# Attention's first batch in two halves, FFN from the 58th step, and a weight fetch moved behind keys

## The chip, the core and the metric

The kernel runs on one core of one Trainium2 chip. The metric is the device time of one execution in microseconds, here the median of three runs. TensorE does the matrix products and the transposes (through an identity matrix), VectorE and ScalarE the elementwise work, GpSimd some elementwise work on data in SBUF, and SyncE (SP) issues nearly all DMAs, in the order of its queue. Each engine runs its own instructions in order.

## What is computed

A sparse attention over 8 batches and 8 heads (each of 512 local positions sees 32 neighbours on both sides and 32 global positions; the global positions see all), and an FFN with an ELU over its 4608 rows.

```python
s_ll = np.where(abs(i - j) <= 32, scale * q_l @ k_l.T, -1e9)
s_l = np.concatenate([scale * q_l @ k_g.T, s_ll], axis=-1)
out_l = sm(s_l) @ np.concatenate([v_g, v_l])          # 512 local rows
out_g = sm(scale * q_g @ k_all.T) @ v_all             # 32 global rows
x = concat([out_g, out_l]).transpose(0, 2, 1, 3).reshape(4608, 512)
h = x @ w_in                                          # 512 -> 2048
g = np.where(h > 0, h, np.exp(np.minimum(h, 0)) - 1)
return g @ w_out                                      # 2048 -> 512
```

Inputs are float32; the FFN weights come as raw 64-bit words and the kernel makes pairs of float16 numbers (a high and a low part) of them. An FFN product is three float16 products: high x high, low x high, high x low.

## The kernel before

**Attention** is a generator. It goes through slots: a "g" slot (`stage_ga`: scores and exponentials of the global rows of one group of four heads) or an "l" slot (a tile: 128 local positions of four heads). For a tile `stage_s` makes the scores (L769 on TensorE, L780 on VectorE with mask and minimum), then exponentials (`ex`, L786, ScalarE) and the norm (L790 and L791 on VectorE, L793 four times on GpSimd, L795 on VectorE). `stage_t` transposes (L809) and copies (L811), `stage_u` transposes the global part (L742 to L745) and copies it (L746, L748, L750 on ScalarE), and `stage_v` multiplies with the values (L853, L822) and copies the result into `xr` (L859 on ScalarE, L864 to L868 on VectorE). Each slot gives four steps. Scores run up to three slots ahead of values. Two "half blocks" of 256 positions make up a batch; `finish` says that one is ready when both groups of heads have their two tiles of that half. A ready half block is split into float16 parts `xh` (L568, ScalarE) and `xl` (L571, VectorE).

**Weights** come in 16 parts of 1 MB (`fetch`, tile `raw`, of which there are two buffers), alternately of w_in (m = 0) and w_out (m = 1). `unit` turns one part into float16: L188 (ScalarE), L189 (GpSimd), L193, L196, L200 (VectorE), L204 (ScalarE, which sums and frees the raw tile), a maximum over partitions (L141), then L213 (ScalarE) and L216 (VectorE). Parts are gathered in groups a (part pair 0), b (1), c (2, 3), d (4 to 7), and f (all 8); `tables` makes a group's scale factors some steps after its last part.

**FFN** is a second generator. A block is done in four jobs by groups a to d while weights are missing, each adding its partial result to an HBM buffer `od` (L440, L459, L455), or in one job f, whose second product uses seven quarter products instead of eight. First product: L324; activation: L333, L334, L335 on ScalarE, L342 on VectorE, split in L349 (ScalarE) and L345 (VectorE); second product: L447 or L482.

What sets the order is a loop over attention's steps with a table of pace: from the step in `PACE[1]` on, FFN pieces (six matmuls each) are put between attention's steps, 180 of them by step 112, 850 by step 320. `UNITS` are the steps at which the first weight parts are started; from eight steps ahead of FFN's start on, credits start the rest. A scheduler then sets the final place of each instruction on its engine, by priorities in that order.

Of the kernel before, what the change touches and what calls it, by code (L numbers as in the profile page):

```python
# [23 lines left out]
NT = SL // P  # L24
# [12 lines left out]
AHEAD = 2  # L37


PACE = ((0, 0), (66, 0), (112, 180), (320, 850))  # L40
WARM = 10
CONV = 14
NBL = B * SL // BLK
GROUPS = {"a": (0, 1), "b": (1, 2), "c": (2, 4), "d": (4, 8), "f": (0, 8)}
BEHIND = 60
UNITS = 0, 1, 8, 18, 30
NX = 4


# [11 lines left out]
def attn_ffn(ctx: ExitStack, tc: tile.TileContext, qT, qgT, kT, vT, vgT, vpT, w_in, w_out, mask, out):  # L61
# [23 lines left out]
    def defer(n, fn):  # L85
        if n == 0:
            return fn()
        later.setdefault(now[0] + n, []).append(fn)
# [49 lines left out]
    def all_max(dst, src):  # L138

        tp = ps_a.tile([P, 512], F32, name="pa")  # L140
        tc.keep_in_program_order(nc.tensor.transpose(tp[:, 0:P], src.to_broadcast([P, P]), ident))  # L141
        nc.vector.tensor_reduce(out=dst, in_=tp[:, 0:P], op=ALU.max, axis=AX.X)
# [15 lines left out]
    def load_weights():  # L158
        todo = [(group, m, p) for group in "abcd" for p in range(*GROUPS[group]) for m in range(2)]
        raws = [fetch(*todo[0][1:])]  # L160
        yield
        for n, (group, m, p) in enumerate(todo):
            if n + 1 < len(todo):
                raws.append(fetch(*todo[n + 1][1:]))
            unit(m, p, raws[n])
            if (m, p) == (1, GROUPS[group][1] - 1):
                defer(12, lambda group=group: tables(group))
                if p == NP - 1:
                    defer(13, lambda: tables("f"))
            yield  # L170

    def fetch(m, p):
        raw = ffn.tile([P, NC, 2 * P, 2] if m == 0 else [P, 2, DM, 2], I32, name="raw")
        nc.sync.dma_start(raw, w1[:, :, 2 * p * P:2 * (p + 1) * P, :] if m == 0 else w2[:, 2 * p:2 * p + 2, :, :])
        return raw
# [51 lines left out]
    def tables(group):  # L227

        r = slice(*GROUPS[group])
        wm = wts.tile([P, 4], F32, name=f"wm_{group}")  # L230
        t = wts.tile([P, NP], F32, name=f"t_{group}")
        nc.vector.tensor_mul(t[:, r], pww[:, r], pwo[:, r])
        nc.vector.tensor_reduce(out=wm[:, 0:1], in_=t[:, r], op=ALU.max, axis=AX.X)

        def rest():
            all_max(wm[:, 1:2], wm[:, 0:1])
            nc.vector.reciprocal(wm[:, 2:3], wm[:, 1:2])
            nc.vector.tensor_scalar(t[:, r], pwo[:, r], wm[:, 2:3], 8.0, ALU.mult, ALU.mult)
            nc.vector.tensor_scalar_mul(isc[:, r], pww[:, r], -2.0 ** -28)
            tab[group] = wm[:, 1:2], t  # L240

        defer(5, rest)
# [417 lines left out]
    def attention():  # L660
# [251 lines left out]

        slots = []
        for b in range(B):
            if b == 0:
                slots += [(*a, *t) for g in range(2) for a, t in [(("g", b, g), ())] + [(("l", b, g), (t,)) for t in range(NT)]]
                continue
            body = [("l", b, g, t) for h in range(2) for g in range(2) for t in (2 * h, 2 * h + 1)]
            slots += [("g", b, 0)] + body[:2] + [("g", b, 1)] + body[2:]
        sts = [{"b": b} for b in range(B)]  # L920
# [28 lines left out]
        for i in range(n + LAGT + 1):  # L949
# [13 lines left out]
            for what in "SVTU" if i < switch else "TSUV":  # L963
# [7 lines left out]
                elif what == "V":  # L971
                    if pairs:
                        b, g, half = pairs.pop()
# [9 lines left out]

    f = ffn_stream()
    units = load_weights()
    done = credit = 0

    def pace(i):
        for (i0, d0), (i1, d1) in zip(PACE, PACE[1:]):
            if i < i1:  # L990
                break
        return d0 + (d1 - d0) * (i - i0) / (i1 - i0)

    def convert(n):
        nonlocal credit
        credit += n
        if credit >= CONV:
            credit -= CONV
            next(units, None)

    for i, _ in enumerate(attention()):
        lead[0] = i < PACE[1][0]
        if i in UNITS:
            next(units)
        elif i >= PACE[1][0] - 8:
            convert(2)
        want = pace(i)
        if lead[0]:
            next(f)
        if done >= want:  # L1010
            tick()
        while done < want:
            if next(f):
                tick()
                break
            done += 1
            convert(1)
            tick()
# [55 lines left out]
```

## Time and profile before

| what | value |
|---|---|
| median of three runs (lowest, highest) | 953.72 us (953.09, 955.16) |
| profiled execution: time, span | 954.72 us, 952.9 us |
| granted TensorE clock, mean | 0.977 |
| busy, TensorE / weight loads | 908.5 us (95%) / 727.8 us (76%) |
| busy, VectorE / ScalarE / GpSimd | 728.1 (76%) / 670.1 (70%) / 271.1 us (28%) |
| HBM read, written | 70.89 MB, 15.20 MB |

Shares of a whole span mix stages with different limits, so the stages are read apart below. In the rows, `x4` behind a form is a count, `[1.5 <-ACT xh L568]` is idle time of the engine ahead of the instruction and the instruction that ended it.

### The profile page before, as it was taken

The numbers are of one execution on the slowest core, as the hardware profiler recorded it, in microseconds if no ns is written. First come the engines' busy times: TensorE is split into PE (matmuls) and PEld (weight loads), VectorE is DVE, ScalarE is ACT, GpSimd is POOL, SyncE is SP. The second block draws the span as 40 slices with busy tenths as digits, with TensorE's granted clock in tenths as the row PEclk, the third lists the DMA queues.
The fourth block names the chain that finished last, engine by engine and source line by source line (L and its number), as shares of the span: only waits on it lengthen the run. The fifth ranks groups of instructions, "written<-read, shape, count | busy, mean of one in ns | idle before, by whom it ended". The sixth has DMA issues, their size and how long they took to land.

```text
span 952.9 us, 23830 instructions
## 1 busy us (share of the span) xinstructions
PE 908.5 (95%) x9216; PEld 727.8 (76%) x9216; DVE 728.1 (76%) x2025; ACT 670.1 (70%) x1584; POOL 271.1 (28%) x483
## 2 busy tenths in 40 slices
PE   6889887899999999999999999999999999999997
PEld 3567564566666788888888888888888888888886
DVE  4988988889967777768776877687777777676566
ACT  5888996776656767757677767677767767666564
POOL 4655481461522322122121212221332312100000
PEclk8779999899999999999999999999999999999999
DMA  6855876331342023101330123102310101000000
GB/s 262 299 179 180 282 224 191 124 123 57 115 157 90 23 100 103 47 26 46 105 121 26 46 78 125 47 27 79 122 49 25 46 23 35 2 23 23 1 24 23
DMA packets 41769, 87.64 MB, mean 92 GB/s; under 512 B 7736, under 2 KB 8888, under 8 KB 41656
## 3 DMA queue, kind: packets, MB, share of 16 engines
q1 hardware_dynamic: 41368, 85.85, 26.6%
q8 instruction: 73, 1.20, 0.5%
q14 instruction: 40, 0.33, 0.1%
q10 hardware_dynamic: 288, 0.26, 0.1%
HBM read 70.89 MB, written 15.20 MB: 90 GB/s over the span
## 4 chain that ended last, share of the span: by engine, by line
PE 67%; DVE 14%; ACT 9%; POOL 3%; issue 3%; DMA 3%; SPq 0%; DVEq 0%; ACTq 0%; POOLq 0%
PE pa L324 25%; PE acc L482 12%; PE h L482 9%; PE acc L447 4%; PE pa L822 3%; PE h L324 3%; PE pa L769 3%; PE pa L809 2%; ACT p L786 2%; DMA raw<-w_out 2%; PE pa L889 2%; DVE gl L345 1%; POOL p L793 1%; DVE cu L196 1%; DVE cu L200 1%
## 5 line engine op out<-in xcount | busy, mean ns | idle before, releaser
L324 PEld LDWEIGHTS <-winh 128*128 128x128 f16 x2160 | 209.4, 98 | 39.2 <-issue 8.4
L793 POOL TENSOR_SCALAR p<-p,sm 128x128 f32<-128x128 f32 x256 | 147.8, 593 | 303.2 <-DVE sm L791 165.0
L324 PE MATMUL pa<-xh,winh 128*128 128x256 f16 x824 | 224.9, 273 | 0.1
L324 PE MATMUL pa<-xl,winh 128*128 128x256 f16 x824 | 224.6, 273 | 0.0
L324 PE MATMUL pa<-xh,winl 128*128 128x256 f16 x824 | 224.6, 273 | 0.0
L361 ACT ACTIVATE gh<-gx,xs 128x896 f16<-128x896 f32 x103 | 107.3, 1042 | 123.1 <-DVE gx L358 123.0
L345 DVE SCALAR_TENSOR_TENSOR gl<-gx,xs,gh 128x896 f16<-128x896 f32 x103 | 119.4, 1159 | 59.9 <-ACT gh L361 59.0
L482 PEld LDWEIGHTS <-gh 128*128 128x128 f16 x1456 | 139.5, 98 | 24.0 <-issue 7.4
L786 ACT ACTIVATE p<-p,m 128x160 f32<-128x160 f32 x256 | 106.7, 421 | 41.6 <-DVE m L780 41.4
L324 PEld LDWEIGHTS <-winl 128*128 128x128 f16 x1080 | 106.1, 98 | 14.3 <-issue 1.2
L333 ACT ACTIVATE g<-pa,xs 128x512 f32<-128x512 f32 x103 | 70.3, 682 | 24.4 <-PE pa L324 23.8
L482 PE MATMUL acc<-wouth,gh 128*128 128x256 f16 x312 | 85.2, 273 | 0.0
L482 PE MATMUL acc<-woutl,gh 128*128 128x256 f16 x312 | 85.1, 273 | 0.0
L335 ACT ACTIVATE g<-g 128x512 f32<-128x512 f32 x135 | 85.0, 630 | 0.1
L482 PE MATMUL acc<-wouth,gl 128*128 128x256 f16 x312 | 85.0, 273 | 0.0
L482 PEld LDWEIGHTS <-gl 128*128 128x128 f16 x728 | 71.2, 98 | 9.2 <-DVE gl L345 1.0
L482 PE MATMUL h<-raw,gh 128*128 128x256 f16 x416 | 75.0, 273 | 0.0
L324 PE MATMUL h<-xh,winh 128*128 128x256 f16 x256 | 71.1, 279 | 1.5 <-ACT hs L334 0.9
L324 PE MATMUL h<-xl,winh 128*128 128x256 f16 x256 | 71.0, 278 | 0.7 <-DVE xl L571 0.7
L324 PE MATMUL h<-xh,winl 128*128 128x256 f16 x256 | 71.0, 278 | 0.0
L780 DVE CUSTOM_DVE_ANT_0 p<-pa,msk 128x160 f32<-128x160 f32 x228 | 61.5, 318 | 4.8 <-PE pa L769 4.7
L342 DVE SCALAR_TENSOR_TENSOR gx<-g,hs 128x512 f32<-128x512 f32 x51 | 35.9, 704 | 36.0 <-ACT g L335 35.6
(236 smaller groups left out, 2016.9 us busy)
## 6 DMA issues: line engine op xcount, KB each, us to landing
k<-kT SPq DMA_DIRECT2D x32, 640.0 KB, 5.1
v<-vT SPq DMA_DIRECT2D x64, 256.0 KB, 2.8
q<-qT SPq DMA_DIRECT2D x32, 256.0 KB, 5.6
raw<-w_in SPq DMA_DIRECT2D x8, 1024.0 KB, 5.9
raw<-w_out SPq DMA_DIRECT2D x8, 1024.0 KB, 6.8
out<-o SPq DMA_DIRECT2D x32, 256.0 KB, 2.3
od<-o SPq DMA_DIRECT2D x24, 256.0 KB, 3.1
o<-od SPq DMA_DIRECT2D x24, 256.0 KB, 2.8
```

The source lines that it names most:

```text
L324: nc.tensor.matmul(h[:, j, :], wt[:, c, f], xt[:, c, :], start=k == 0, stop=k == 11)
L333: nc.scalar.activation(g, hf, AF.Relu, scale=sc[:, p:p + 1])
L335: nc.scalar.activation(g, g, AF.Exp, scale=-1.0)
L342: nc.vector.scalar_tensor_tensor(out=out, in0=ins[0], scalar=-1.0, in1=ins[1], op0=ALU.add, op1=ALU.max)
L345: nc.vector.scalar_tensor_tensor(out=dst, in0=src, scalar=sg, in1=hi, op0=ALU.mult, op1=ALU.subtract)
L361: nc.scalar.activation(gh, gx, AF.Copy, scale=sg)
L447: nc.tensor.matmul(acc[t], gt[:, s], wt[:, f, :], start=p == first and j == 0 and k == 0, stop=p == last and j == 1 and k == 2)
L482: nc.tensor.matmul(cols, gt, w, start=p == 0 and k == 0, stop=last and k == len(todo) - 1, skip_group_check=True)
L769: nc.tensor.matmul(sp[r][half * HQ:(half + 1) * HQ, j * KW:(j + 1) * KW], q[rows, qs], k[rows, t, half, :], start=True, stop=True)
L780: nc.vector.tensor_tensor_reduce(out=p, in0=sp[r][:, j * KW:(j + 1) * KW], in1=msk[:, mi, :], op0=ALU.add, op1=ALU.min, scale=-scale, scal ...
L786: nc.scalar.activation(ps[i], ps[i], AF.Exp, bias=m[:, i:i + 1], scale=-1.0, accum_out=s[:, 0, i:i + 1])
L793: nc.gpsimd.tensor_scalar(ps[i][:, 0:P], ps[i][:, 0:P], s[:, 1, i:i + 1], 1.0, ALU.mult, ALU.mult)
```

## The change

Attention's first batch did its two groups of heads one after the other, four tiles each. Now it goes like the others: two tiles of the first group, two of the second (first half), then the same for the second half. FFN starts at step 58 instead of 66, weight parts are started at steps 0, 5, 9, 18, 30, and the scale tables are made four steps later after their group's last part.

```diff
-PACE = ((0, 0), (66, 0), (112, 180), (320, 850))
+PACE = ((0, 0), (58, 0), (112, 180), (320, 850))
...
-UNITS = 0, 1, 8, 18, 30
+UNITS = 0, 5, 9, 18, 30
...
-                defer(12, lambda group=group: tables(group))
+                defer(16, lambda group=group: tables(group))
                 if p == NP - 1:
-                    defer(13, lambda: tables("f"))
+                    defer(17, lambda: tables("f"))
...
         for b in range(B):
-            if b == 0:
-                slots += [(*a, *t) for g in range(2) for a, t in [(("g", b, g), ())] + [(("l", b, g), (t,)) for t in range(NT)]]
-                continue
             body = [("l", b, g, t) for h in range(2) for g in range(2) for t in (2 * h, 2 * h + 1)]
             slots += [("g", b, 0)] + body[:2] + [("g", b, 1)] + body[2:]
```

What stands on the queue of SP right after the mask's load, before the change (`raw` are weight parts, `v` values, `q` queries, `k` keys, `qg` global queries, `ptw2` the global values of a group):

```order
L174 DMA raw_164<-w_in 128x4x512
L174 DMA raw_166<-w_out 128x2x1024
L688 DMA ptw2_83<-vpT 128x256
L681 DMA v_200<-vT 128x512
L681 DMA v_237<-vT 128x512
L676 DMA qg_254<-qgT 128x64
L666 DMA k_256<-kT 128x1280
L666 DMA k_258<-kT 128x1280
L174 DMA raw_231<-w_in 128x4x512
```

and after it:

```order
L174 DMA raw_164<-w_in 128x4x512
L676 DMA qg_174<-qgT 128x64
L666 DMA k_176<-kT 128x1280
L666 DMA k_178<-kT 128x1280
L688 DMA ptw2_83<-vpT 128x256
L681 DMA v_197<-vT 128x512
L174 DMA raw_199<-w_out 128x2x1024
L671 DMA q_219<-qT 128x512
L671 DMA q_221<-qT 128x512
L681 DMA v_240<-vT 128x512
L174 DMA raw_242<-w_in 128x4x512
```

The second weight part has moved behind the second group's keys, and that group's queries, which stood behind the third part, now stand ahead of it.

ScalarE from the first tile's exponentials (`p1_94`) on, before; `p2_95` and `p0_93` are the second and the third tile:

```order
L786 ACTIVATE p1_94,sm_193<-p1_94,m_192 128x160 x4
L188 ACTIVATE cu_168<-raw_164 128x1024
L786 ACTIVATE p2_95,sm_226<-p2_95,m_225 128x160 x4
L786 ACTIVATE p0_93,sm_271<-p0_93,m_270 128x160 x2
L188 ACTIVATE cu_233<-raw_166 128x1024
L786 ACTIVATE p0_93,sm_271<-p0_93,m_270 128x160 x2
L746 COPY ptw0_81<-pa_289 64x4x32
L748 COPY ptw0_81<-pa_289 64x4x32
L750 COPY ptg0_84<-pa_289 128x2x64
L786 ACTIVATE p1_94,sm_320<-p1_94,m_319 128x160
L204 ACTIVATE raw_164,cm_169<-cu_168 128x1024
```

and after:

```order
L786 ACTIVATE p1_94,sm_191<-p1_94,m_190 128x160 x4
L188 ACTIVATE cu_201<-raw_164 128x1024
L786 ACTIVATE p2_95,sm_234<-p2_95,m_233 128x160 x4
L204 ACTIVATE raw_164,cm_202<-cu_201 128x1024
L746 COPY ptw0_81<-pa_303 64x4x32
L748 COPY ptw0_81<-pa_303 64x4x32
L750 COPY ptg0_84<-pa_303 128x2x64
L720 ACTIVATE pg_277,sg_279<-pa_263,mg_278 128x4x64
L720 ACTIVATE pg_277,sg_279<-pa_264,mg_278 128x4x64
L722 ACTIVATE pu_280,sg_279<-pa_263,mg_278 128x32
L859 COPY xr_327<-h_329 128x2x128
L188 ACTIVATE cu_244<-raw_199 128x1024
```

The third tile's exponentials have gone from between the second tile and the first L204; L204 now follows the second tile directly, and the second part's L188 stands behind the first tile's value copy L859.

ScalarE further on, ahead of FFN, before; `xh_762` is the first half block, `raw_1080` the sixth weight part:

```order
L786 ACTIVATE p1_94,sm_860<-p1_94,m_859 128x160 x2
L859 COPY xr_478<-h_869 128x2x128
L786 ACTIVATE p1_94,sm_860<-p1_94,m_859 128x160 x2
L188 ACTIVATE cu_1192<-raw_1080 128x1024
L568 ACTIVATE xh_762<-xr_329,xm_330 128x1024
L720 ACTIVATE pg_917,sg_919<-pa_903,mg_918 128x4x64
```

and after (`xh_610`, `raw_968`):

```order
L568 ACTIVATE xh_610<-xr_327,xm_328 128x1024
L786 ACTIVATE p0_93,sm_792<-p0_93,m_791 128x160
L859 COPY xr_658<-h_797 128x2x128
L786 ACTIVATE p0_93,sm_792<-p0_93,m_791 128x160 x2
L746 COPY ptw1_82<-pa_830 64x4x32
L748 COPY ptw1_82<-pa_830 64x4x32
L750 COPY ptg1_85<-pa_830 128x2x64
L188 ACTIVATE cu_1102<-raw_968 128x1024
```

The split L568 of the first half block has gone from behind the sixth part's L188 to seven rows ahead of it.

## Prediction

> **What bounds the kernel now.** The view by stages comes first. Its rows give for a stretch its length, then the busy time (and count) of TensorE (PE), of the weight loads (PEld), of VectorE (DVE), ScalarE (ACT) and GpSimd (POOL), the granted TensorE clock, the DMA share and GB/s.
>
> ```profile
> 0.00:17.00 17.00, 11.12 (x92) 5.72 (x92) 5.47 (x35) 8.23 (x29) 6.84 (x22) 0.95 0.89 335
> 17.00:50.00 33.00, 26.17 (x249) 17.71 (x247) 30.35 (x113) 25.25 (x78) 21.02 (x34) 0.71 0.73 259
> 50.00:77.00 27.00, 23.72 (x296) 17.10 (x293) 21.18 (x98) 20.53 (x75) 16.95 (x44) 0.82 0.45 142
> 77.00:140.00 63.00, 56.47 (x523) 39.39 (x522) 55.98 (x153) 58.91 (x137) 35.63 (x52) 1.00 0.72 241
> 140.00:200.00 60.00, 50.66 (x369) 32.03 (x368) 50.63 (x125) 45.58 (x94) 24.42 (x40) 0.91 0.46 145
> 200.00:233.00 33.00, 31.41 (x264) 21.57 (x263) 30.99 (x59) 20.45 (x40) 8.70 (x12) 1.00 0.27 89
> 267.00:900.00 633.00, 628.73 (x6717) 530.00 (x6715) 467.16 (x1299) 438.25 (x1024) 140.06 (x266) 1.00 0.17 58
> ```
>
> From 267 us TensorE is busy 628.73 of 633. In 17-50 VectorE is the fullest (30.35 of 33); in 77-140 ScalarE is (58.91 of 63), VectorE just behind; in 50-77 no engine is full, and VectorE lacks 5.8 us. Next the chain of work that ended last, read for where TensorE takes over:
>
> ```profile
> 232.62 0.68 DVE o L455
> 233.33 2.78 PE acc L447 x12
> ...
> 243.44 1.97 PE h L324 x18
> ```
>
> Up to 233 us the chain runs mostly over VectorE and ScalarE, then it is TensorE alone. In the order of instructions the two kernels are the same on TensorE from the 780th of 5808 FFN matmuls on, which stands at about 243 us here. So the change is worth what it shifts the arrival at that matmul; the 710 us behind it stay.
>
> **What stays the same.** Each engine issues the same instructions in both, but for one L811 copy that goes from VectorE to ScalarE. So the sum is one of order and waiting. The stall that can be won stands in the timeline of VectorE (start, length, line, and in brackets the idle time ahead with what ended it):
>
> ```profile
> 66.79 2.14 DVE L571 SCALAR_TENSOR_TENSOR xl<-xr,xm,xh 128x1024 f16<-128x1024 f32 x1 [1.52 <-ACT xh L568]
> 73.58 0.23 DVE L864 COPY xglob<-h 128x64 f32<-128x64 f32 x1 [1.51 <-ACT xr L859]
> 85.33 0.75 DVE L345 SCALAR_TENSOR_TENSOR gl<-g,xs,gh 128x512 f16<-128x512 f32 x1 [1.20 <-ACT gh L349]
> 87.41 0.76 DVE L342 SCALAR_TENSOR_TENSOR g<-g,hs 128x512 f32<-128x512 f32 x1 [1.03 <-ACT g L335]
> ```
>
> **Term 1, the first 50 us: +2.5 us.** The timelines of ScalarE, GpSimd, VectorE and TensorE:
>
> ```profile
> 12.88 1.11 ACT L188 ACTIVATE cu<-raw 128x1024 f32<-128x1024 f32 x1
> 15.65 1.04 POOL L189 TENSOR_SCALAR cu<-cu 128x1024 f32<-128x1024 f32 x1
> 12.07 0.30 DVE L780 CUSTOM_DVE_ANT_0 p<-acc,msk 128x160 f32<-128x160 f32 x1
> 16.72 0.69 DVE L193 TENSOR_SCALAR cu<-cu 128x1024 int32<-128x1024 int32 x1 [2.86 <-POOL cu L189]
> 18.83 1.22 DVE L196 SCALAR_TENSOR_TENSOR cu<-raw,cu 128x1024 int32<-128x1024 int32 x1
> 20.28 1.22 DVE L200 SCALAR_TENSOR_TENSOR cu<-raw,cu 128x1024 int32<-128x1024 int32 x1
> 46.20 1.21 DVE L200 SCALAR_TENSOR_TENSOR cu<-raw,cu 128x1024 int32<-128x1024 int32 x1
> 22.42 0.80 PE L853 MATMUL h<-ptg,ptw 128*64 128x160 f32 x4 [2.98 <-DVE ptg L753]
> 24.18 0.85 PE L822 MATMUL h<-ptw,v 128*64 128x96 f32 x8
> 112.23 1.41 POOL L793 TENSOR_SCALAR p<-p,sm 128x128 f32<-128x128 f32 x4
> ```
>
> Now the scores of four tiles need only the first group's keys, and the third tile's L780 run at 12.07, ahead of VectorE's wait for L189. After the change tile 3 needs queries that stand on SP's queue behind the second weight part, and ScalarE has L204 of the first part right behind tile 2. That L204 waits: L189 comes about 0.35 us later (one more L793 ahead of it, a quarter of the 1.41 at 112.23), L193, L196 and L200 follow (0.6 + 1.1 + 1.2), so ScalarE stands empty from about 15.5 to 20. VectorE then runs dry: its next conversion step waits for the first tile's values on TensorE (22.42 to about 25 now), then the copy L859, the moved L188 (1.0, as from 12.88) and L189 (1.04); I count two gaps near 23.4 and 25.5, 3.3 us in all, as an estimate from those durations. About 1 us of present gaps there goes (VectorE idles 2.65 us in all in 17-50). Taking all, the fourth weight part's L200, which starts at 46.20 now, starts some 2.5 us later with the same eight score tiles done. Bounds: 0, if queries come in time and the gaps fill; +4, the two gaps and the 1 us of tile 3's L780 (4 x 0.25) with nothing gone. I take the middle, as the order puts a wait at each place.
>
> **Term 2, the stall in 62-74 us: -3.0 us.** SP's issues and ScalarE's:
>
> ```profile
> 22.79 0.38 SPq L174 DMA_DIRECT2D raw<-w_in  x1
> 38.51 0.38 SPq L174 DMA_DIRECT2D raw<-w_in  x1
> 56.99 0.38 SPq L174 DMA_DIRECT2D raw<-w_out  x1
> 64.60 1.13 ACT L188 ACTIVATE cu<-raw 128x1024 f32<-128x1024 f32 x1 [1.61 <-DMA raw<-w_out]
> 65.63 1.13 ACT L568 ACTIVATE xh<-xr,xm 128x1024 f16<-128x1024 f32 x1
> ```
>
> The sixth weight part, issued at 56.99, holds ScalarE until 64.60; behind that L188 stands L568, for which VectorE's L571 waits, and the ninth tile's copies. After the change L568 of the first block stands seven rows ahead of that L188, and a full stop of ScalarE there no longer holds it. The two gaps of 1.52 and 1.51 are this term. Bounds: 0, if they come back elsewhere; -5, most of the 5.8 us that VectorE lacks in 50-77.
>
> **Term 3, FFN two score tiles earlier: -5.2 + 4.4 us.** Where FFN starts, and the groups of instructions up to 77 us (busy us, mean ns):
>
> ```profile
> 77.15 0.27 PE L324 MATMUL h<-xh,winh 128*128 128x256 f16 x1
> L786 ACT ACTIVATE p<-p,m 128x160 f32<-128x160 f32 x48 | 20.0, 423 | 2.4 <-DVE m L780 2.4
> L780 DVE CUSTOM_DVE_ANT_0 p<-pa,msk 128x160 f32<-128x160 f32 x24 | 7.0, 311 | 0.0
> L811 DVE COPY ptw<-pa 128x512 f32<-128x512 f32 x10 | 6.8, 681 | 0.8 <-PE pa L809 0.8
> L868 DVE TENSOR_REDUCE xm<-xr 128x1 f32<-128x256 f32 x10 | 4.1, 409 | 0.0
> L859 ACT COPY xr<-h 128x256 f32<-128x256 f32 x10 | 3.7, 370 | 5.3 <-PE h L822 5.1
> L571 DVE SCALAR_TENSOR_TENSOR xl<-xr,xm,xh 128x1024 f16<-128x1024 f32 x2 | 3.4, 1708 | 1.5 <-ACT xh L568 1.5
> L750 ACT COPY ptg<-pa 128x128 f32<-128x128 f32 x10 | 2.6, 265 | 0.2
> ```
>
> By the order, 11 score tiles and 9 value tiles stand ahead of the first L324 (13 and 10 now). Lengths overlap by 0.07 to 0.1 where instructions follow each other, so I take that much off. VectorE has less ahead of it by 2 x (4 x 0.25 + 0.35) = 2.7 for scores and norms (the norms an estimate), 0.6 + 0.33 + 0.33 = 1.26 for L811, L868 and two smaller ones of one tile, and 1.2 for one L571 (the 2.14 at 66.79 was the longer of the two): 5.2 us. With terms 1 and 2 the first L324 comes at 77.15 + 2.5 - 3.0 - 5.2 = 71.5. What was put off is done in 77-140, where ScalarE is at 94%: 8 L786 at 0.41, three copies like L750 0.8, one L859 0.3 = 4.4 us. VectorE's 5.2 is the other bound, 4.0 (without the L571, which fits a gap) the lower. I take ScalarE's, the fuller engine.
>
> **Term 4, the first pieces: -1.0 us.** The gaps of 1.20 and 1.03 are VectorE waiting for the first pieces' exponentials, with little else queued. With tiles still open, and weight conversion started at step 50 instead of 58 (the fifth part's L193 now stands ahead of the first L342 by several rows more), they fill partly. Bounds 0 and -2.
>
> Edits at no cost of their own: UNITS 0, 5, 9 and the tables' 16 and 17 steps are in the order that terms 1 and 3 read; the tables of group a stand some 100 rows of VectorE ahead of FFN's first, which covers their four steps, and the cover goes only if term 1 were several times its size. PACE meets the old line again at step 112.
>
> Sum: +2.5 - 3.0 - 5.2 + 4.4 - 1.0 = -2.3 us. The profiled execution took 954.72 us with a span of 952.9 (1.8 around it), 1.0 above the median of 953.72; the sum is a difference and is taken from the median: 951.4.
>
> GpSimd's L793 of a later tile, to be held against the four in 1.41 us above:
>
> ```profile
> 127.27 3.82 POOL L793 TENSOR_SCALAR p<-p,sm 128x128 f32<-128x128 f32 x3
> ```
>
> [...]
>
> **Rivals.** *Nothing changes (chance 0.33).* Either 77-140 is full on ScalarE, and what FFN gains by starting at 71 is spent there: with VectorE's 5.2 in term 3 and term 4 at 0, the sum is +2.5 - 3.0 = -0.5: 953.2 (0.25). Or four L793 of the second tile, which now have the conversion's L200 beside them, take the 3.8 us of 127.27 for 1.4, term 1 is 2.4 more and the sum +0.1: 953.8 (0.08). For it: the same instructions on engines at 89% and 94%. Against: VectorE still idles 7 us there.
>
> *The early starvation stays (chance 0.24), slower.* Place: ScalarE's row L204 behind tile 2, and VectorE waiting for L189. Price: +4.0 in term 1; the stalls of term 2 return, since the sixth part is only fetched when the fourth is converted, which is late itself: 0. Then +4.0 - 5.2 + 4.4 = +3.2: 956.9. It decides once the eighth score tile is more than 4 us later than now. For it: SP hands out each part only when a buffer frees (issues at 22.79 and 38.51 follow the L204 of two parts earlier). Against: between the fourth part's L200 (done at 47.4) and the sixth's issue at 56.99 lie over 9 us now.
>
> Part of that rival (0.06) is the clock, in the view by stretches of 10 us:
>
> ```profile
> 30.00:40.00 10.00, 8.48 (x115) 6.14 (x115) 9.04 (x35) 8.42 (x28) 4.51 (x10) 0.96 0.72 243
> 40.00:50.00 10.00, 9.50 (x62) 6.32 (x62) 9.31 (x43) 8.07 (x28) 8.32 (x14) 0.50 0.96 344
> ```
>
> At clock 0.50 TensorE gets 62 matmuls done in the time of 115; one more such stretch on the path to the first L324 delays it by up to 4.9 us (62 x (9.50/62 - 8.48/115)), though mostly beside VectorE. [...]
>
> **How the numbers follow.** My forecast, a gain of more than 0.2% (1.9 us, about what a measurement can tell), has 0.43, its own range 946.5 to 951.8; nothing 0.33; slower 0.24. The ends of the terms give -8.2 (0 - 5 - 5.2 + 4.0 - 2) and +4.0 (+4 + 0 - 5.2 + 5.2 + 0). The range 947.0 to 957.5 leaves out the last piece at the low end and what passes +3.8 at the high one, about 2 in 10 in all.
>
> **What would show it.** Right: first L324 between 70 and 74 us; gaps of VectorE near 23 and 26 us; no wait for a weight part at 64; the first L345 and L342 waiting less than 2 us together; the handover to TensorE near 231. Wrong: the first L324 later than 75, or the units so bunched behind it that VectorE's idle time in 77-140 exceeds 7 us; then the time lies above 953.

## The result: 1.3% slower, and the profile after

| what | before | after |
|---|---|---|
| median of six runs beside each other (lowest, highest) | 953.45 us (950.02, 955.67) | 963.73 us (963.08, 965.13) |
| ratio, 95% interval | | 1.0132 (1.0106 to 1.0158) |
| profiled execution: time, span, mean clock | 954.72, 952.9 us, 0.977 | 964.04, 962.2 us, 0.978 |
| VectorE busy / TensorE busy | 728.1 / 908.5 us | 732.1 / 904.8 us |

The forecast was 951.4 us in a range of 947.0 to 957.5. The change costs 10 us by these two medians (their quotient is 1.0108) and 12.6 us by the ratio. The ratios here and below are of fast runs alone and are not the quotients of the medians shown; three disturbed runs of the experiments (968.05, 1835.87 and 2405.69 us) are not in them. The view by stages of the kernel after, with the columns as in the prediction:

```profile
0.00:17.00 17.00, 9.67 (x79) 4.23 (x82) 4.29 (x26) 6.86 (x24) 6.81 (x22) 0.86 0.87 316
17.00:50.00 33.00, 20.30 (x188) 14.12 (x182) 23.55 (x82) 19.78 (x61) 15.40 (x27) 0.66 0.61 215
50.00:77.00 27.00, 21.66 (x302) 15.71 (x301) 24.93 (x112) 22.45 (x79) 16.08 (x34) 1.00 0.56 191
77.00:140.00 63.00, 55.82 (x537) 38.59 (x536) 55.38 (x168) 57.42 (x143) 37.66 (x65) 0.93 0.68 230
140.00:200.00 60.00, 50.15 (x400) 30.92 (x399) 52.69 (x122) 46.98 (x96) 25.46 (x31) 0.96 0.52 165
```

VectorE (the third pair) is empty for 33.00 - 23.55 = 9.45 us in 17-50, where it was empty for 2.65; in 50-77 it is empty for 2.07 instead of 5.82. In 77-140 the idle time is 7.6 us, as before (7.0). So the loss stands in the first 50 us, and some of it is won back in the stall that the change did remove.

The timelines say where. TensorE first, then VectorE with one row of ScalarE (start, length, line, idle time ahead and what ended it):

```profile
15.22 1.07 PE L703 MATMUL pa<-k,qg 64*32 64x256 f32 x4 [5.85 <-DMA k<-kT]
22.27 0.88 PE L809 MATMUL pa<-ident,p 128*128 128x128 f32 x4 [2.49 <-DVE mg L716]
38.51 0.47 PE L809 MATMUL pa<-ident,p 128*128 128x128 f32 x1 [1.89 <-POOL p L793]
45.98 1.29 PE L769 MATMUL acc<-k,q 64*64 64x160 f32 x6 [2.63 <-DVE t_a L232]
77.45 0.27 PE L324 MATMUL h<-xh,winh 128*128 128x256 f16 x1
```

```profile
17.36 0.69 DVE L193 TENSOR_SCALAR cu<-cu 128x1024 int32<-128x1024 int32 x1 [3.52 <-POOL cu L189]
20.60 1.13 ACT L204 ACTIVATE raw<-cu 128x1024 f32<-128x1024 f32 x1 [4.85 <-DVE cu L200]
26.15 0.22 DVE L864 COPY xglob<-h 128x64 f32<-128x64 f32 x1 [1.82 <-ACT xr L859]
28.35 0.69 DVE L193 TENSOR_SCALAR cu<-cu 128x1024 int32<-128x1024 int32 x1 [1.65 <-POOL cu L189]
43.02 1.28 DVE L216 SCALAR_TENSOR_TENSOR winl<-cu,cm,winh 128x1024 f16<-128x1024 f32 x1 [3.33 <-ACT winh L213]
54.62 1.93 DVE L200 SCALAR_TENSOR_TENSOR cu<-raw,cu 128x1024 int32<-128x1024 int32 x1
58.90 0.31 DVE L780 CUSTOM_DVE_ANT_0 p<-pa,msk 128x160 f32<-128x160 f32 x1
```

The last row is the last L780 of the eighth score tile; before, that instruction stood at 49.08. Of these 9.8 us, 8.1 are more idle time of VectorE up to that row (22.3 instead of 14.2 us, summed over its timeline) and 1.7 are more work that stands ahead of it. The fourth weight part's L200, 46.20 before, stands at 54.62. The chain of waits through 34 to 44 us shows the piece that the prediction did not have in its sum (start, length, what):

```profile
34.83 5.02 POOL p L793 x4
...
39.89 0.47 PE pa L809
...
41.10 0.27 ACT ptw L746
...
41.94 1.06 ACT winh L213
...
43.02 1.28 DVE winl L216
```

Four L793 of the third tile, the first of the second group, take 5.02 us on GpSimd (1.41 in a row of the prediction), with VectorE's conversion of the third part beside them. TensorE's transposes come one by one behind them, ScalarE's copies and L213 behind those, and VectorE waits 3.33 us for L213. Such slow L793 are not new. In the kernel before, the same tile's four took 1.51 us, but the next tile's took 4.14:

```profile
41.02 1.51 POOL L793 TENSOR_SCALAR p<-p,sm 128x128 f32<-128x128 f32 x4 [0.54 <-ACT p L786]
43.51 4.14 POOL L793 TENSOR_SCALAR p<-p,sm 128x128 f32<-128x128 f32 x4 [0.97 <-DVE sm L791]
```

What is new is that they now stand on the chain of waits.

FFN's first L324 comes at 77.45, where it stood at 77.15, with five L780 fewer begun ahead of it (44 instead of 49; four make a score tile). The eleventh score tile is 7.0 us late, and lateness of that size is carried to the handover to TensorE: by the records of the two traces the 780th FFN matmul comes 7.2 us later and those from about the 1000th on 8.9 us later, which is the difference of the two spans (9.3) to within 0.4.

### The profile page after: what moved, and what is told of

Read it like the earlier page. It is cut to its first block, busy times and chain, and to the rows that moved or that the text cites. A ratio compares the mean times of both kernels' runs of the same rounds, so it can differ in the third digit from the quotient of the medians.

```text
span 962.2 us, 23830 instructions
## 1 busy us (share of the span) xinstructions
PE 904.8 (94%) x9216; PEld 724.9 (75%) x9216; DVE 732.1 (76%) x2024; ACT 671.9 (70%) x1585; POOL 261.9 (27%) x483
## 4 chain that ended last, share of the span: by engine, by line
PE 65%; DVE 15%; ACT 12%; issue 3%; POOL 3%; DMA 3%; SPq 0%; DVEq 0%; ACTq 0%; POOLq 0%
PE pa L324 25%; PE acc L482 12%; PE h L482 9%; PE acc L447 3%; PE pa L822 3%; PE pa L769 3%; PE h L324 2%; PE pa L809 2%; ACT p L786 2%; POOL p L793 2%; DVE gl L345 2%; PE pa L889 2%; DVE cu L275 1%; ACT raw L204 1%; ACT g L333 1%
## 5 line engine op out<-in xcount | busy, mean ns | idle before, releaser
L324 PEld LDWEIGHTS <-winh 128*128 128x128 f16 x2160 | 208.3, 98 | 39.7 <-issue 9.2
L793 POOL TENSOR_SCALAR p<-p,sm 128x128 f32<-128x128 f32 x256 | 137.1, 553 | 335.9 <-DVE sm L791 203.4
L324 PE MATMUL pa<-xh,winh 128*128 128x256 f16 x824 | 224.9, 273 | 0.1
L324 PE MATMUL pa<-xl,winh 128*128 128x256 f16 x824 | 224.6, 273 | 0.0
L324 PE MATMUL pa<-xh,winl 128*128 128x256 f16 x824 | 224.6, 273 | 0.0
L345 DVE SCALAR_TENSOR_TENSOR gl<-gx,xs,gh 128x896 f16<-128x896 f32 x103 | 119.9, 1164 | 60.0 <-ACT gh L361 59.1
L324 PEld LDWEIGHTS <-winl 128*128 128x128 f16 x1080 | 105.8, 98 | 13.5 <-DVE winl L216 0.8
L333 ACT ACTIVATE g<-pa,xs 128x512 f32<-128x512 f32 x103 | 70.4, 683 | 24.1 <-PE pa L324 23.5
L324 PE MATMUL h<-xh,winh 128*128 128x256 f16 x256 | 70.0, 274 | 1.6 <-ACT xh L568 1.6
L324 PE MATMUL h<-xh,winl 128*128 128x256 f16 x256 | 69.9, 273 | 0.3 <-DVE winl L216 0.3
L324 PE MATMUL h<-xl,winh 128*128 128x256 f16 x256 | 70.0, 273 | 0.0
L780 DVE CUSTOM_DVE_ANT_0 p<-pa,msk 128x160 f32<-128x160 f32 x232 | 62.3, 317 | 4.5 <-PE pa L769 4.4
L342 DVE SCALAR_TENSOR_TENSOR gx<-g,hs 128x512 f32<-128x512 f32 x51 | 35.9, 705 | 35.9 <-ACT g L335 35.5
```

The source lines that it names most:

```text
L324: nc.tensor.matmul(h[:, j, :], wt[:, c, f], xt[:, c, :], start=k == 0, stop=k == 11)
L333: nc.scalar.activation(g, hf, AF.Relu, scale=sc[:, p:p + 1])
L342: nc.vector.scalar_tensor_tensor(out=out, in0=ins[0], scalar=-1.0, in1=ins[1], op0=ALU.add, op1=ALU.max)
L345: nc.vector.scalar_tensor_tensor(out=dst, in0=src, scalar=sg, in1=hi, op0=ALU.mult, op1=ALU.subtract)
L780: nc.vector.tensor_tensor_reduce(out=p, in0=sp[r][:, j * KW:(j + 1) * KW], in1=msk[:, mi, :], op0=ALU.add, op1=ALU.min, scale=-scale, scal ...
L793: nc.gpsimd.tensor_scalar(ps[i][:, 0:P], ps[i][:, 0:P], s[:, 1, i:i + 1], 1.0, ALU.mult, ALU.mult)
```

## The experiments

In the expectations "piece 58" is step 58 of attention's loop, and the four runs of one group were timed beside runs of the kernel before on the same chip. The medians of before in the four groups were 949.68, 952.59, 951.91 and 950.71 us, so ratios are compared, not times. The expectations give times for a kernel before at 953.45 us; a ratio times that is 1 to 4 us more than the time measured in its group. One table first, with landmarks from the timelines: the start of the last L780 of the eighth and of the eleventh score tile, the first L324, and the 1st, 9th and 21st L342 on VectorE (the 21st is close to the handover; in the three kernels with other steps for the weight parts and FFN from 66 it is the 22nd that stands as far from the end, some 716 us, and it is given in its place).

| kernel | ratio (95%) | tile 8 | tile 11 | L324 | L342: 1st, 9th, 21st |
|---|---|---|---|---|---|
| before | 1 | 49.1 | 69.9 | 77.2 | 83.3, 146.9, 237.2 |
| before, second trace | 0.9991 (0.9968 to 1.0015) | 49.5 | 70.2 | 78.1 | 84.4, 148.8, 234.8 |
| halves alone | 1.0111 (1.0079 to 1.0144) | 55.5 | 76.7 | 85.1 | 90.8, 154.1, 240.4 |
| halves, three tiles first, alone | 1.0085 (1.0058 to 1.0113) | 54.3 | 74.4 | 81.7 | 86.7, 155.1, 240.2 |
| weight parts alone | 1.0096 (1.0066 to 1.0126) | 52.0 | 71.7 | 80.5 | 87.0, 154.1, 241.3 |
| second part alone | 1.0065 (1.0041 to 1.0089) | 52.3 | 70.6 | 79.4 | 84.3, 151.4, 239.4 |
| FFN from 58 alone | 1.0126 (1.0092 to 1.0160) | 49.1 | 70.0 | 74.2 | 81.0, 150.3, 248.0 |
| FFN from 58, old rate, alone | 1.0131 (1.0096 to 1.0166) | 49.2 | 70.4 | 75.0 | 81.8, 150.5, 246.2 |
| parts + FFN from 58 | 1.0076 (1.0049 to 1.0102) | 52.3 | 70.7 | 71.6 | 78.6, 153.0, 237.5 |
| same, late conversion | 1.0078 (1.0054 to 1.0103) | 52.1 | 71.7 | 72.6 | 77.3, 150.9, 240.9 |
| halves + FFN from 58 + tables' steps | 1.0085 (1.0056 to 1.0114) | 55.3 | 73.3 | 73.9 | 81.0, 156.5, 240.2 |
| halves + parts | 1.0143 (1.0108 to 1.0178) | 58.4 | 77.6 | 85.8 | 90.6, 158.0, 243.8 |
| after (all three) | 1.0132 (1.0106 to 1.0158) | 58.9 | 76.9 | 77.5 | 84.6, 161.1, 245.8 |
| after, second qg buffer | 1.0137 (1.0108 to 1.0165) | 59.0 | 77.0 | 77.5 | 84.6, 161.2, 246.0 |
| after, three tiles first | 1.0085 (1.0061 to 1.0108) | 54.3 | 74.9 | 75.8 | 82.9, 158.2, 243.6 |
| after, all eight tiles' L793 on VectorE | 1.0120 (1.0089 to 1.0152) | 56.5 | 79.2 | 79.8 | 86.9, 161.8, 247.5 |
| after, third tile's L793 on VectorE | 1.0100 (1.0070 to 1.0131) | 56.4 | 75.1 | 75.7 | 82.8, 158.8, 242.2 |
| after, late conversion | 1.0149 (1.0112 to 1.0187) | 58.4 | 77.9 | 79.8 | 84.4, 156.5, 246.3 |

**One part undone or done alone.**

The half-by-half order undone in the kernel after:

```diff
         for b in range(B):
+            if b == 0:
+                slots += [(*a, *t) for g in range(2) for a, t in [(("g", b, g), ())] + [(("l", b, g), (t,)) for t in range(NT)]]
+                continue
```

> The changed kernel with one part undone: the first batch again goes group by group, all four tiles of the first group ahead of the second group's keys; FFN still from piece 58, weight parts still at 0, 5, 9. Theory A (the half-by-half order of the first batch starves the first 50 us: TensorE waits 5.85 us for the second group's keys, and the third tile's four L793 on GpSimd take 5.0 us beside VectorE's conversion) expects the loss gone: 950 to 955 us, the eighth score tile back to its old time and the first L324 near 73 us. Rival B (FFN from piece 58 crowds 77-140 us, whatever stands before it) expects 961 to 964 us still. Rival C (the second weight part behind the keys makes all later parts late) expects 959 to 964 us, with the fourth part's fetch still near 33 us (26.2 before, 33.4 after).

Measured 956.91 us, ratio 1.0076: between the theories by its time; for a before at 953.45 it would be 960.7, inside theory C's range. The first L324 comes at 71.58, earlier than either kernel:

```profile
71.58 0.27 PE L324 MATMUL h<-xh,winh 128*128 128x256 f16 x1
52.27 0.31 DVE L780 CUSTOM_DVE_ANT_0 p<-pa,msk 128x160 f32<-128x160 f32 x1
```

That is the forecast's number (71.5), but by luck: it was forecast for the half-by-half order, with terms 1 and 2 in it. And it brings nothing: the 5.6 us by which L324 is early against before are gone at the ninth L342 (153.0 against 146.9). The half-by-half order on top of this costs 1.0132 - 1.0076, some 0.55%.

The half-by-half order alone, in the kernel before:

```diff
-            if b == 0:
-                slots += ...
-                continue
```

> The kernel before with the first batch half by half and nothing else changed: weight parts at 0, 1, 8, FFN from piece 66. Theory A expects nearly the whole loss: 959 to 964 us, the first L324 at 82 to 86 us instead of 77.15. Rival B (pacing) and rival C (weight parts) both expect 952 to 955.5 us, as before.

960.50 us, ratio 1.0111, first L324 at 85.11: theory A's number. The eighth tile is 6.4 us late and the eleventh 6.8.

```profile
55.47 0.32 DVE L780 CUSTOM_DVE_ANT_0 p<-pa,msk 128x160 f32<-128x160 f32 x1
17.17 1.52 DVE L193 TENSOR_SCALAR cu<-cu 128x1024 int32<-128x1024 int32 x1 [3.50 <-POOL cu L189]
31.47 0.29 DVE L142 TENSOR_REDUCE cm<-pa 128x1 f32<-128x128 f32 x1 [1.74 <-PE pa L141]
21.24 1.15 ACT L204 ACTIVATE raw<-cu 128x1024 f32<-128x1024 f32 x1 [4.65 <-DVE cu L200]
```

FFN from step 58 alone:

```diff
-PACE = ((0, 0), (66, 0), (112, 180), (320, 850))
+PACE = ((0, 0), (58, 0), (112, 180), (320, 850))
```

> The kernel before with FFN from piece 58 alone: old order of the first batch, weight parts at 0, 1, 8. Theory A expects no loss: 950 to 954 us, the first L324 at 71 to 74 us. Rival B expects 959 to 964 us, with the time lost between 77 and 140 us. Rival C expects 951 to 955 us.

961.54 us, ratio 1.0126: rival B's time, against theory A, though not where B put it. L324 comes 3.0 us earlier, the ninth L342 3.4 us later, and the 21st 10.8 (the traced execution took 966.43; in the run at the old rate below, traced at 963.51, it is 9.0). Between about 150 and 205 us VectorE waits for TensorE's scores, and one score tile more stands there than before (16 L780 instead of 12 in 147-192). The groups by line of VectorE in 150-205 (busy us, mean ns, idle time ahead and what ended it):

```profile
L780 DVE CUSTOM_DVE_ANT_0 p<-pa,msk 128x160 f32<-128x160 f32 x16 | 4.8, 318 | 3.9 <-PE pa L769 3.8
```

The stretch itself, with TensorE's granted clock at 0.81:

```profile
150.00:205.00 55.00, 47.80 (x370) 29.93 (x368) 40.18 (x125) 39.39 (x95) 19.59 (x34) 0.81 0.40 130
```

The weight parts and the tables' steps alone:

```diff
-UNITS = 0, 1, 8, 18, 30
+UNITS = 0, 5, 9, 18, 30
...
-                defer(12, lambda group=group: tables(group))
+                defer(16, lambda group=group: tables(group))
...
-                    defer(13, lambda: tables("f"))
+                    defer(17, lambda: tables("f"))
```

> The kernel before with the weight parts at 0, 5, 9 and the tables' 16 and 17 steps alone. Theory A expects little: 952 to 956 us. Rival C expects 957 to 964 us, with the fourth part's fetch 4 to 7 us later than 26.2 us and the first L324 as much later. Rival B expects 953 to 955 us.

958.96 us, ratio 1.0096, theory C's time, though the fourth part's fetch, at 29.33 us (26.22 before), is 3.1 us late and not 4 to 7; the first L324 is 3.3 us late. So none of the three theories alone: each part costs about 1% by itself. Theory A was too narrow; its place (the first 50 us) holds for two of the three parts: at the eighth tile the halves alone are late by 6.4 us, the parts by 3.0, FFN from 58 by nothing, and all three by 9.8. There the costs add up, and VectorE's idle time grows by 4.2 us with the halves alone, by 1.7 with the parts and by 8.1 with all three. In the time of the whole kernel the costs do not add up (1.0111, 1.0096 and 1.0126 against 1.0132 together).

The kernel after with FFN from 66 again (`PACE` as before):

> The changed kernel with FFN from piece 66 again: half-by-half first batch, weight parts at 0, 5, 9. If the parts' costs added up (half by half alone gave a ratio of 1.0111, the parts alone 1.0096), the ratio would be 1.021 and the first L324 near 88 us. If each of the three parts spends the same slack (VectorE and ScalarE fill up to the handover near 235 us, so only the idle time that a part adds there is lost), the ratio is 1.008 to 1.014 as with all three.

964.26 us, ratio 1.0143: not the sum, and just above the second reading's edge. The eighth tile is at 58.4 as in after.

The kernel after with `UNITS` 0, 1, 8 again. The expectation speaks of the tables' steps 12 and 13 as well, but the edit leaves them at 16 and 17:

```diff
-UNITS = 0, 5, 9, 18, 30
+UNITS = 0, 1, 8, 18, 30
```

> The changed kernel with the weight parts at 0, 1, 8 and the tables' 12 and 13 steps again: half-by-half first batch, FFN from piece 58. If the costs added up (1.0111 and 1.0126), 1.024. If they spend the same slack, 1.008 to 1.014. If the second weight part's place behind the keys is what makes up for the half-by-half order, more than 1.015, with the first L703 of the second group later than 15.22 us.

958.81 us, ratio 1.0085; within "the same slack", and against the guess that the second part's place makes up for the half-by-half order. L703 of the second group runs at 16.13 here, 0.9 us later than in after, and the time is still better. The eighth tile is at 55.3, as with the halves alone (55.5), so the tables' later steps, which are in here, do not delay it.

**Which wait carries the first 50 us.**

A second place for the second group's global queries, so that SP need not stop at 3.95 to 8.12 us:

```diff
-            qg = apool.tile([P, 2, SG], F32, name="qg", bufs=1)
+            if (b, g) == (0, 1):
+                qg = apool.tile([P, NC, SG], F32, name="xg", bufs=1)[:, 0:2, :]
+            else:
+                qg = apool.tile([P, 2, SG], F32, name="qg", bufs=1)
```

> The changed kernel with a second buffer for the global queries of the first batch's second group (in space that is used only later), so that SP needn't stop from 3.95 to 8.12 us for the first group's last L703. If that stop is what makes the second group's keys late (TensorE's wait of 5.85 us at 15.22), the keys' L703 runs near 12 us, the third tile 3 us sooner, and the time is 957 to 961 us. If the DMA queues are full anyway (316 GB/s in 0-17 us), L703 moves by less than 1 us and the time stays at 962 to 965 us.

964.06 us, ratio 1.0137: no effect, though for neither reason given. L703 does come earlier, by 1.6 us, and the next transposes come where they came:

```profile
13.65 1.07 PE L706 MATMUL pa<-k,xg 64*32 64x256 f32 x4 [4.20 <-DVE sm L794]
22.23 0.93 PE L812 MATMUL pa<-ident,p 128*128 128x128 f32 x4 [3.49 <-DVE mg L719]
```

(Lines are three further down here.) The wait for the keys is hidden behind VectorE, whose maximum of the second group's scores (L716 of after) stands behind the conversion of the first part, and that waits for L189. TensorE's longest wait on the page was not the one to shorten.

L793 of the first batch's eight tiles on VectorE:

```diff
-                    nc.gpsimd.tensor_scalar(ps[i][:, 0:P], ...)
+                    (nc.vector if early else nc.gpsimd).tensor_scalar(ps[i][:, 0:P], ...)
```

with `early = st["b"] == 0`.

> The changed kernel with the first batch's L793 on VectorE instead of GpSimd. If GpSimd's 5.02 us for the third tile's four L793 (34.83 to 39.9 us) beside VectorE's conversion is a cause of the loss, VectorE does them in some 1 us per tile, ScalarE's L746 at 41.10 no longer waits 3.39 us, the fourth weight part's L200 comes 2 to 3 us sooner than 54.62, and the time is 958 to 961.5 us. If the wait for the keys alone sets that stretch, 962 to 966 us, since VectorE has some 8 us more to do before the first L324.

962.19 us, ratio 1.0120: by its time at the lower edge of the second reading. But the eighth tile is 2.4 us earlier than in after and the eleventh 2.3 us later, where VectorE pays for the other tiles. So the third tile's was moved alone, `early = (st["b"], g, t) == (0, 1, 0)`:

> The changed kernel with the four L793 of one tile alone, the first of the second group, on VectorE instead of GpSimd, where they took 5.02 us beside the conversion. With all eight tiles of the batch there the eighth score tile was done at 56.8 us instead of 59.2, but VectorE had more to do later. If GpSimd beside VectorE is a cause, the eighth tile is done at 56.5 to 57.5 us, the eleventh near 75 (77.2), and the time is 960.5 to 962.5 us. If not, the eighth tile comes within 0.7 us of 59.2 and the time is 963 to 965 us.

961.56 us, ratio 1.0100 (after 1.0132); tiles and time as the first reading has them (56.4 and 75.1; the profiled execution took 960.11 against 964.04), though for a before at 953.45 the time would be 963.0, at the second reading's edge. The last L780 of the eighth tile, and GpSimd's next L793 (one line further down here):

```profile
56.44 0.31 DVE L780 CUSTOM_DVE_ANT_0 p<-pa,msk 128x160 f32<-128x160 f32 x1
39.36 3.58 POOL L794 TENSOR_SCALAR p<-p,sm 128x128 f32<-128x128 f32 x4 [5.94 <-PE pa L744]
```

GpSimd beside VectorE's conversion is worth about 2.5 us of the 9.8 at the eighth tile and some 3 us of the end. The intervals of the two ratios overlap; the landmarks carry this, not the median. Not all of it is gone: the fourth tile's four L793 now take 3.58 us. Whether the same move would gain as much in the kernel before was not run.

Three tiles of the first group ahead of the second group's keys, in the kernel after:

```diff
+            if b == 0:
+                slots += [("g", 0, 0), *(("l", 0, 0, t) for t in range(3)), ("g", 0, 1), ("l", 0, 1, 0), ("l", 0, 1, 1),
+                          ("l", 0, 0, 3), ("l", 0, 1, 2), ("l", 0, 1, 3)]
+                continue
```

> The changed kernel with one more score tile of the first batch ahead of the second group's keys: three tiles of the first group, the second group's keys, its first two tiles, the first group's fourth, the last two. Theory: half by half leaves VectorE with the scores of only two tiles in the window in which it waits for the first weight part (up to 17.4 us), and the other tiles then stand where it is full; its idle time ahead of the first L342 is 24.4 us with the change and 17.8 with the old order. Then one tile back brings part of these 6.6 us: 959 to 962 us, idle 20 to 23. If the loss lies elsewhere in the half-by-half order (the second group's keys, GpSimd beside VectorE), 963 to 966 us.

960.18 us, ratio 1.0085, first reading: VectorE's idle time ahead of the first L342 is 22.7 us, the eighth tile at 54.3, 4.6 us earlier. The same order in the kernel before:

> The kernel before with the first batch nearly half by half: three tiles of the first group, the second group's keys, its two tiles, the first group's fourth, the last two; nothing else changed. If the half-by-half order costs by the tiles that it takes from ahead of the second group's keys, the eighth score tile, at 55.8 us with two tiles first and 49.4 with four, is done at 51 to 53 us and the time is 953 to 957 us. If it costs by the second group's keys and tiles being in the way at all, 55 to 56 us and 958 to 962 us.

958.53 us, ratio 1.0085, the eighth tile at 54.3: nearer the second reading. One tile back brings 1.1 us of the 6.4 at the eighth tile here, 4.6 in the kernel after. Of the 6.4 us of the halves alone, 4.2 are more idle time of VectorE and 2.2 more work ahead of the tile. In its rows shown above the first weight part's L193 waits 3.50 us for GpSimd's L189 (2.86 before), ScalarE's L204 4.65 us for VectorE behind that, and L142 1.74 us for TensorE; which of them makes the others was not taken apart further.

The second weight part's step alone, 5 instead of 1, with the tables' steps 16 and 17 (`UNITS = 0, 5, 8, 18, 30`):

> The kernel before with the second weight part's step at 5 instead of 1 and the tables' steps 16 and 17 alone; the third part stays at 8. All parts' moves together delayed the eighth score tile by 3.0 us (49.4 to 52.3) and gave a ratio of 1.0096. If the second part's place carries that, the tile is done at 51.5 to 52.5 us and the ratio is 1.005 to 1.010; if it is the third part's place, 49.2 to 50.2 us and 0.998 to 1.003.

958.58 us, ratio 1.0065, the eighth tile at 52.3: the second part's place, with the tables' steps that go with it, carries all that the parts cost there (3.2 us; 3.0 with the third part moved too), and by the run of the kernel after with `UNITS` 0, 1, 8 it is not the tables' steps. VectorE waits for L204 of the part that was put off:

```profile
29.67 0.15 DVE L131 TENSOR_SCALAR pwo<-cm 128x1 int32<-128x1 int32 x1 [1.98 <-ACT raw L204]
```

**Why the earlier FFN brings nothing.**

The change of `PACE` also starts the conversion's credits eight steps earlier. That undone in the kernel after:

```diff
-        elif i >= PACE[1][0] - 8:
+        elif i >= PACE[1][0]:
```

> The changed kernel with the conversion of weights between pieces started at piece 58, where it started before, instead of at 50, which the change of the pace moved as well. Theory F: with FFN from 58 the conversion runs ahead of FFN; between the fifth and the ninth L342 VectorE does 15.2 us of conversion instead of 10.5, and the weights' sums (24.6 us before, 28.6 after) come ahead of TensorE's handover, which they needn't. Started later, the stretch from the first L342 to the ninth is shorter by 3 to 5 us and the time 958.5 to 961.5 us. Rival: VectorE only has the same work in another order, 962 to 966 us.

964.02 us, ratio 1.0149: theory F falls. VectorE's conversion between the fifth and ninth L342 is 10.5 us again and its sums of weights up to the 21st are 22.4 instead of 28.6, as foreseen, but its idle time up to there grows by as much (49.6 us against 43.2). With the old order of the first batch, the same:

> The same late start of the conversion with the first batch group by group as before: what is left of the change is FFN from piece 58 and the weight parts at 0, 5, 9. Theory F expects 951 to 955 us, against 956.9 with the early start; the rival 956 to 959 us.

958.85 us, ratio 1.0078, the rival's number by its time, and nearly the ratio that the early start gave (1.0076).

FFN from 58 at the old rate, in the kernel before:

```diff
-PACE = ((0, 0), (66, 0), (112, 180), (320, 850))
+PACE = ((0, 0), (58, 0), (104, 180), (320, 850))
```

> The kernel before with FFN from piece 58 and its 180 steps up to piece 104 instead of 112: the old rate, eight pieces earlier. If FFN from 58 costs because the flatter rate puts attention and conversion between the first pieces (the stretch from the first to the ninth L342 was 69 to 77 us with it, 63.6 before), that stretch is 62 to 66 us and the time 947 to 953 us. If the work up to the handover is the same in any order, what is put off comes later, and the time is 954 to 962 us.

963.51 us, ratio 1.0131; the stretch from the first to the ninth L342 is 68.7 us, as with the flatter rate (69.3), and the time is above both ranges. The rate is not it; the early start is, of FFN and of the conversion that starts with it.

The kernel before once more, unchanged:

> The kernel before, unchanged, for a second trace of it. Its times so far lie in two groups, near 948.8 and near 954.5 us, and the trace that the prediction rests on took 954.72. That trace shows TensorE empty for 3.52 us at 158 to 162 us and its granted clock at 0.57 behind that, and the stretch from the ninth to the thirteenth L342 took 45.0 us where the same instructions took 41.3 us with the half-by-half order alone. If that halved clock is the difference, a run near 949 us has no halved clock in 160 to 170 us and a stretch of 40 to 42 us; in a run near 954.5 us it is there again.

The profiled execution took 952.48 us, 951.24 is the median. The same wait in the two traces, first in the prediction's, then in the second one (TensorE's timeline; behind each the view by stretches, with the clock third from the end):

```profile
161.80 0.32 PE L141 MATMUL pa<-ident,cm 128*128 128x128 f32 x1 [3.52 <-ACT raw L204]
```

```profile
162.00:166.00 4.00, 4.00 (x31) 2.46 (x30) 3.95 (x17) 1.14 (x3) 0.00 (x0) 0.57 0.88 239
```

```profile
161.08 0.32 PE L141 MATMUL pa<-ident,cm 128*128 128x128 f32 x1 [0.83 <-ACT raw L204]
```

```profile
162.00:166.00 4.00, 4.00 (x46) 2.46 (x46) 3.95 (x16) 3.11 (x5) 0.00 (x0) 1.00 0.90 261
```

After a gap of 3.52 us the clock is 0.57 and TensorE gets 31 matmuls done in 4 us; after one of 0.83 it is 1.00, with 46. The ninth to the thirteenth L342 take 45.0 us in the one and 41.0 in the other. But 2.7 of these 4.0 us stand between the tenth and the eleventh L342 (6.6 and 3.9 us), around the gap itself, so the clock behind it can make 1.3 at most. The gap goes back to a weight part that ScalarE waits for, 3.09 us in the prediction's trace and 0.33 in the second:

```profile
158.91 1.12 ACT L188 ACTIVATE cu<-raw 128x1024 f32<-128x1024 f32 x1 [3.09 <-DMA raw<-w_out]
```

```profile
158.12 1.18 ACT L188 ACTIVATE cu<-raw 128x1024 f32<-128x1024 f32 x1 [0.33 <-DMA raw<-w_out]
```

So the expectation's halved clock is there in the one and not in the other, but the late weight part is the larger share. Why it came later is open. The second trace is 2.4 us later up to the fifth L342, with a lower clock in places of its own (0.84 in 100-110, 1.00 in the first trace), so its time falls between the two groups of the expectation, and whether the groups come from this one stretch stays open. What is shown: the prediction's trace holds some 4 us there that another execution of the same kernel does not have.

## Why the prediction was wrong, point by point

**Term 1 (+2.5, bounds 0 to +4) is the step that failed most.** All it named is there: ScalarE's empty stretch ends with an L204 that waited 4.85 us at 20.60, and the two gaps of VectorE are at 26.15 and 28.35, 3.5 us together (3.3 foreseen, near 23.4 and 25.5). What it took as unchanged behind them was not: the third tile's scores now fall beside the conversion, with 5.02 us of L793 and 3.33 us of VectorE's waiting, and the second part's place alone puts off the eighth tile by 3.2 us (3.0 with the third part's). The term's own landmark, the fourth part's L200, moved by 8.4 us. It was mis-sized because it added up the gaps at the start, which are 3.5 of the 8.1 us by which VectorE's idle time grows up to the eighth tile, and assumed the rest of the 50 us to be as full as before and to hold the same work. The edits of `UNITS` and the tables' steps, which the prediction put at no cost of their own, cost 0.65% with the second part's step alone and 0.96% with the third's as well.

**Term 2 (-3.0) was right.** The waits of L571 (1.52) and of L864 (1.51) are gone from the kernel after:

```profile
67.47 1.30 DVE L571 SCALAR_TENSOR_TENSOR xl<-xr,xm,xh 128x1024 f16<-128x1024 f32 x1
78.19 0.21 DVE L864 COPY xglob<-h 128x64 f32<-128x64 f32 x1
```

The lateness of 9.8 us at the eighth tile is 7.0 at the eleventh: 2.8 us won. Without the change of `PACE` it only goes from 9.3 to 7.7, so part of it hangs on `PACE`.

**Term 3 (-5.2 + 4.4): the first half held, the second was too small.** In the kernel after, the first L324 follows the eleventh tile's last L780 by 0.5 us, where it followed by 7.2. With the first batch as before and the rest of the change in, it came at 71.58. But what is put off is paid back in full by the ninth L342, which comes 6.1 us late there: between the first and the ninth VectorE has 3.2 us more of L780 to do, as the prediction saw, and 5.7 us more of weight conversion, whose earlier start it named in term 4 but gave no price here; the same step of the table starts both. By the 21st this kernel stands at 237.5 us, before at 237.2 and 234.8. From the eleventh tile to the 21st L342 the runs with FFN from 58 and another part take 167 to 169 us, those from 66 take 164 to 170; the gain of 1.8 us (term 3 with term 4) is in neither. In after it is 168.9 us against 167.2, so that the account at the 21st L342 is 9.8 - 2.8 + 1.7 = 8.7 us late, where the forecast had 2.5 - 3.0 - 1.8 = -2.3. On top of another part FFN from 58 lowers the ratio by 0.1 to 0.3%, less than the intervals can tell. FFN from 58 alone loses 1.3%; one score tile and its waits then stand in 150-205 us, but why they cost so much more there than with the other parts of the change is not settled.

**Term 4 (-1.0) came nearly in size.** The first L345 waits 1.40 us and no L342 of the first pieces does (1.20 and 1.03 before), 0.8 us less:

```profile
86.70 0.78 DVE L345 SCALAR_TENSOR_TENSOR gl<-g,xs,gh 128x512 f16<-128x512 f32 x1 [1.40 <-ACT gh L349]
90.21 0.68 DVE L342 SCALAR_TENSOR_TENSOR g<-g,hs 128x512 f32<-128x512 f32 x1
```

As with term 3, nothing of it reaches the handover.

**The base.** The median of the three runs shown, 953.72, lies above all four later medians of before (949.68 to 952.59), and the trace holds some 4 us near 162 us that the second trace doesn't, with a late weight part and a lowered clock. No term was taken from that stretch, and the ratio does not contain it; in time it is at most 0.5%, and not what made the sign wrong.

**The rivals.** "The early starvation stays" (0.24) is what happened: place and wait are as it says, and the eighth score tile, which was to decide at 4 us, is 9.8 us late. Its price was 4 us too small in term 1, and its stall in 62-74 did not return. Its part on the clock did not come: in 17-50 the clock was 0.66 instead of 0.71, but in 50-77 it was 1.00 instead of 0.82. That one more stretch at 0.50 would come was the author's guess; no run shows what lowers the clock. "Nothing changes" through GpSimd's L793 beside VectorE had the kind of loss and its size (2.4 us; the run with the third tile's L793 moved gives 2.5 at the eighth tile) but the wrong tile: it struck the third tile at 34.83, not the second, whose four took 1.58 us at 20.82. The place to look was every tile's L793, not one. What the traces show is four L793 slow beside the conversion (5.02 us for 1.41 here, 4.14 for 1.51 before), not why. Both signs of "wrong" that the prediction named came: the first L324 after 75, and more than 7 us of VectorE's idle time in 77-140 (7.6).

## What to carry to other kernels

Where a first transfer is awaited, count the independent work that stands ahead of it in each engine's order: the change that took some of it away here paid for it in the full stretch behind (9.8 us at the eighth tile, with 3.5 in the gaps at the start), and the landmark to compare is a fixed piece of work some way past the last gap, not the gaps themselves. Starting the next stage sooner brought nothing here, as the same engines had to finish the old one. And before a forecast rests on a trace's gaps, look in a second execution whether they, and the clock behind them, are the kernel's or that execution's (here 3.52 us with 0.57 behind it were 0.83 with 1.00 in the second).

## What the runs showed of the hardware that was not expected

GpSimd and VectorE took longer beside each other, GpSimd the more. Beside VectorE's L795, L193, L216, L196 and L200 between 34.9 and 39.6 us four L793 took 5.02 us instead of 1.41, while the L196 and L200 among these steps kept their usual 1.21. In the other direction there are single places in the same trace: a VectorE L200 took 1.93 us (54.62) instead of 1.21 with a GpSimd L189 beside it that took 2.09 instead of 1.04, and an L795 took 1.12 us instead of the 0.28 at 47.30 with another L189 beside it:

```profile
53.38 2.09 POOL L189 TENSOR_SCALAR cu<-cu 128x1024 f32<-128x1024 f32 x1 [2.44 <-ACT cu L188]
44.22 1.12 DVE L795 TENSOR_TENSOR pz<-p,sm 128x128 f32<-128x128 f32 x1
```

And a low clock of TensorE stood behind gaps of very different lengths. In the two traces of the kernel before, it was at 0.57 for the 4 us behind a gap of 3.52 us and at 1.00 behind one of 0.83. But in the kernel after it was at 0.57 behind a gap of 2.35 us as well:

```profile
137.30 0.39 PE L447 MATMUL acc<-wouth,gh 128*128 128x512 f16 x1 [2.35 <-ACT gh L349]
```

```profile
138.00:142.00 4.00, 4.00 (x13) 1.51 (x12) 3.31 (x6) 3.62 (x5) 3.25 (x5) 0.57 0.95 335
```

And in the prediction's row for 40 to 50 us it was at 0.50 with TensorE busy for 9.50 of 10 us. From 30 to 50 us of that trace TensorE's longest gap is one of 0.74 us, ahead of an L822 at 39.57, while around one of 2.21 us further on the clock was 1.00:

```profile
104.66 0.38 PE L447 MATMUL acc<-wouth,gh 128*128 128x512 f16 x1 [2.21 <-DVE o L455]
```

```profile
100.00:110.00 10.00, 7.38 (x82) 4.20 (x79) 10.00 (x25) 9.44 (x28) 2.96 (x5) 1.00 0.91 321
```

So in these traces the length of a single gap does not decide; what does was not taken apart.
